# The w_down load behind the first gated turn, in two tiles of seven and three row tiles; one store of the last slab whole

## The chip, the cores and the metric

The kernel runs on one core of a Trainium2 chip. The metric is the device time of one execution in microseconds (us). A profile is one execution recorded by the hardware profiler; its span runs from the first to the last instruction.

## What is computed

The input x has 2048 tokens of 512 numbers. It is normalised, and the normalised tokens go two ways: through a diagonal complex linear recurrence over the tokens (an S5 layer with 512 states), and through a gated feed-forward network with 1376 hidden columns. The two results are multiplied and added to x.

```python
xn = layernorm(x)
# S5: h_t = Lam_bar * h_(t-1) + B_bar @ xn_t ;  y = 2 Re(C h) + xn * Dskip
s = A(xn, Lambda, B, C, log_dt, Dskip)
# feed-forward: (gelu(xn @ w_gate) * (xn @ w_up)) @ w_down
g = silu(B(xn, w_gate, w_up, w_down))
out = x + s * g
```

## The kernel before

The tokens are worked on in four slabs of 512 (`NS`), each with four row tiles of 128 tokens (`M`). All weights stay in SBUF: `wg`, `wu` (4 x 128 input rows by 1376 columns), `wd` (11 row tiles of 128 hidden rows, the last with 96, by 512 columns), `BT` and `C2` for the recurrence.

For a row tile, TensorE multiplies by `w_up` and `w_gate` in three column chunks of 512, 512 and 352 (`first_w` in the first slab, `gate_tile`, line 450, in the others); ScalarE takes the results out of PSUM (gelu for the gate), and VectorE multiplies the two into `at` (128 tokens x 1408 columns, `first_at`, lines 445 and 447, in the first slab). A DMA transpose, here called a turn (`at_t`, line 479), writes `at` to `atT` with the hidden index on the partitions. `down_pair` (line 485) then runs eleven matmuls for a row tile over the eleven row tiles of `wd` (line 495), and ScalarE applies silu into `g2` (line 498).

For the recurrence, `half` (line 551) does half of the states of a slab: TensorE multiplies `BT` with the turned normalised tokens `xnT` (line 561), ScalarE copies the results into `U` (line 563), and VectorE rotates, scans (line 592) and rotates back into `hst`. `y_tile` (lines 511 to 527) multiplies `hst` with `C2`, then VectorE multiplies by `g2`, adds x into `ot`, and SP stores the tile. The stores of the last slab's first two row tiles are cut into two halves of 256 columns (line 525).

`norm` (line 759) loads slab s (for s of 2 and 3 through `load_slab`, line 217) and normalises it: ScalarE forms sums (line 774) and writes the normalised tile `xna` (line 779), and one turn for the slab writes `xnT` (line 378).

PSUM has six ring banks, which `bank()` hands out in turn as the steps are built, and two `ybank`s. A matmul group that gets a bank waits until the engine that reads the bank's earlier content is done.

Every piece of work is a numbered step of a `Plan`. A step says what it reads and writes, from which its predecessors follow; its number is its place in the order of building. The list `ORDER` at the head of the file is the order in which steps are issued, written out by hand, and so fixes the order on each engine. All DMAs are issued by SP, in the order of the list, into one hardware queue. In the stretch that matters SP's steps are: turn of `xna` for the first slab, the two turns of `B` into `BT` (steps 15 and 16), `w_down`'s main load of 10 row tiles (step 121, line 695), the turns of the gated row tiles 0, 2 and 1 (steps 160, 162, 161), the turn of the second slab's `xna` (232), the load of the third slab of x (279), the turn of row tile 3 (163), and the two turns of `C` (204, 205). `w_down`'s eleventh row tile (96 rows, step 122, line 696) is loaded early, between weights and the second slab of x.

Of the kernel before, what the change touches and what calls it, by code (L numbers as in the profile page):

```python
# [17 lines left out]
PE, ACT, DVE, POOL, SP = "PE", "ACT", "DVE", "POOL", "SP"  # L18
# [1 line left out]

ORDER = (
# [23 lines left out]
)  # L45


# [33 lines left out]
def kernel(  # L81
# [17 lines left out]
    nc = tc.nc  # L99
    P = 128  # L100
    S = 2048
    D = 512
    F = 1376
# [5 lines left out]
    NS = S // TS  # L109
    M = TS // P  # L110
    NFT = (F + P - 1) // P
    FP = NFT * P
    FL = F - (NFT - 1) * P
    CH = [(0, 512), (512, 1024), (1024, F)]
    HD = D // 2
# [12 lines left out]
    def sb(name, shape, dt=BF16):  # L128
        return consts.tile(shape, dt, name=name)
# [2 lines left out]
    xnT = sb("xnT", [P, 2, M, KT, P])  # L132
    wg = sb("wg", [P, KT, F])
    wu = sb("wu", [P, KT, F])
    wd = sb("wd", [P, NFT, D])
    BT = sb("BT", [P, 2, KT, D])
    C2 = sb("C2", [P, 2, NPT, D])
    pv = sb("pv", [P, P])
# [3 lines left out]
    atT = sb("atT", [P, NFT, TS])  # L142
# [42 lines left out]
    def pe(n, cols, emit, reads=(), writes=(), **kw):  # L185
        return pl.add(PE, n * (cols + 6) / 2400.0, emit, reads, writes, lag=0.22, **kw)
# [4 lines left out]
    def dma(eng, issue, land, emit, reads=(), writes=(), **kw):  # L191
        return pl.add(eng, issue, emit, reads, writes, lag=land, **kw)
# [292 lines left out]
    def down_pair(s, h):  # L485
        gi = g2_n[0] % NG2
        g2_n[0] += 1
        for b in range(2):
            m = 2 * h + b
            r, ps = bank()  # L490

            def f(m=m, ps=ps):
                for k in range(NFT):
                    fs = min(P, F - k * P)
                    T.matmul(ps[:], lhsT=atT[:fs, k, m * P : (m + 1) * P], rhs=wd[:fs, k, :], start=(k == 0), stop=(k == NFT - 1))  # L495
            pe(NFT, 512, f, [("atT", m), "wd0", "wd"], [("bank", r)])
            g2s[s, m] = (gi, b)
            acts(512, lambda b=b, ps=ps: act(out=g2[gi][:, b, :], in_=ps[:], func=AF.Silu), [("bank", r)], [("g2", gi, b)], table="silu", rank=3.0)  # L498

# [2 lines left out]
    def y_part(s, m, c0, c1, bank, key, seed, e):  # L502

        w = c1 - c0
        ps = bank[:, 0:w]
        if seed:
            acts(w, lambda: act(out=ps, in_=sk[s % 2][:, m, c0:c1], func=AF.Copy), [("sk", s % 2, m)], [key])  # L507

        def f():
            for j in range(2 * NPT):  # L510
                T.matmul(ps, lhsT=hst[s % 2][:, j // NPT, j % NPT, m * P : (m + 1) * P], rhs=C2[:, j // NPT, j % NPT, c0:c1],  # L511
                         start=(j == 0 and not seed), stop=(j == 2 * NPT - 1), skip_group_check=True)
        pe(2 * NPT, w, f, [("hst", s % 2, 0), ("hst", s % 2, 1)] + C2S + ([key] if seed else []), [key])
        gi, b = g2s[s, m]
        if seed:
            dve(w, lambda: V.tensor_tensor(out=yg[e][:, c0:c1], in0=ps, in1=g2[gi][:, b, c0:c1], op=ALU.mult), [key, ("g2", gi, b)], [("yg", e, c0)])  # L516
        else:
            ys = tF[:, 0, c0:c1]
            dve(w, lambda: V.tensor_tensor(out=ys, in0=ps, in1=sk[s % 2][:, m, c0:c1], op=ALU.add), [key, ("sk", s % 2, m)], [("tF",)])
            dve(w, lambda: V.tensor_tensor(out=yg[e][:, c0:c1], in0=ys, in1=g2[gi][:, b, c0:c1], op=ALU.mult), [("tF",), ("g2", gi, b)], [("yg", e, c0)])  # L520
        o = 2 + m % 2 if s == NS - 1 and m >= M - 2 else m % 2
        dve(w, lambda: V.tensor_tensor(out=ot[o][:, c0:c1], in0=yg[e][:, c0:c1], in1=x_tok[:, s * M + m, c0:c1], op=ALU.add),  # L522
            [("yg", e, c0), ("x", s, m)], [("ot", o, c0)], rate=2.0)
        mg = s * TS + m * P
        cuts = (0, HD) if (NS - 1, 0) <= (s, m) < (NS - 1, M - 2) else (c0,)
        for lo, hi in zip(cuts, (*cuts[1:], c1)):
            dma(SP, 0.35, 1.5, lambda lo=lo, hi=hi: nc.sync.dma_start(out=out_td[mg : mg + P, lo:hi], in_=ot[o][:, lo:hi]), [("ot", o, c0)], [("out", s, m, lo)], svc=(2, 0.4, 0.9))

# [163 lines left out]
            first_at(m)  # L692
    load_slab(1, after=sp_last)
    wd_r = B_w_down[0 : (NFT - 1) * P, :].rearrange("(k p) d -> p k d", p=P)
    dma(SP, 0.6, 6.7, lambda: nc.sync.dma_start(out=wd[:, 0 : NFT - 1, :], in_=wd_r), writes=["wd0"], after=sp_last, svc=(2, 3.7, 1.0))
    dma(SP, 0.5, 4.0, lambda: nc.sync.dma_start(out=wd[:FL, NFT - 1, :], in_=B_w_down[(NFT - 1) * P : F, :]), writes=["wd"], after=sp_last, svc=(2, 0.3, 1.0))
    dma(SP, 0.7, 3.0, lambda: nc.sync.dma_start(out=Drow[:], in_=A_Dskip.partition_broadcast(P)), writes=["Drow"], after=sp_last, svc=(2, 0.5, 1.0))
    tables()
    for m in range(M):
# [156 lines left out]
```

## Time and profile before

| | us |
|---|---|
| median of three runs (lowest, highest) | 179.38 (179.35, 179.89) |
| the profiled execution | 179.31 |
| its span | 177.5 |
| VectorE busy in the span | 157.5 |
| ScalarE busy in the span | 123.9 |

The profiled execution's own time is 1.8 us more than its span. In the rows of the profile, PE is TensorE's matmuls, PEld its weight loads, DVE is VectorE, ACT ScalarE, POOL GpSimd, and SPq the issue of DMAs by SP. A row of the timeline has the start, the duration, the engine, the line and the operation, the tiles (out<-in), the count of instructions merged into it, and in brackets the idle time of the engine before it with what ended that. A DMA's row there is its issue; the transfer goes on after it. "us to landing" is from the start of the issue to the last byte's signal.

Up to 44 us the queue of DMAs is busy without a long break: weights, turns and three slabs of x go through it. Behind that there are stretches with no transfer at all.

### The profile page before, as it was taken

The page shows a single profiled execution, that of the slowest core. Times are in us where ns is not written, and L with a number is a line of the kernel's source. Part 1 is how long each engine was busy: PE and PEld are TensorE (multiplying, and loading weights), DVE is VectorE, ACT ScalarE, POOL GpSimd, SP SyncE. Part 2 cuts the span into 40 slices and gives each one's busy share as a digit, 9 for nine tenths or more (in the row PEclk, how much of TensorE's full clock was granted, in tenths as well). Part 3 has the DMA queues.
Part 4 walks back from the last instruction along what each step waited for, and adds up shares of the span by engine and source line. Part 5 has one row for each costly group of instructions (what it writes and reads, how often), then busy time and mean ns, then how long its engine had stood idle before and what let it go on. Part 6 is the DMA issues. An engine that isn't in the chain of part 4 may idle for free.

```text
span 177.5 us, 2427 instructions
## 1 busy us (share of the span) xinstructions
PE 172.5 (97%) x846; PEld 82.3 (46%) x846; DVE 157.5 (89%) x256; ACT 123.9 (70%) x238; POOL 11.3 (6%) x26
## 2 busy tenths in 40 slices
PE   8999999899999999999999999999999999999992
PEld 3455453344455544444445454444444455444451
DVE  3678999999699994999979999899999999999754
ACT  6689989839999999899578855373148618572240
POOL 2472030000200000000040000000000000000000
PEclk9999999999999999999999999999999999999999
DMA  5999999999000709414000064094000006626122
GB/s 164 286 344 229 177 264 227 214 265 212 0 0 0 197 3 185 99 61 80 0 0 6 24 135 101 30 192 85 0 0 0 0 30 144 83 52 140 37 62 77
DMA packets 48355, 18.66 MB, mean 105 GB/s; under 512 B 40312, under 2 KB 47832, under 8 KB 48344
## 3 DMA queue, kind: packets, MB, share of 16 engines
q1 hardware_dynamic: 48344, 18.52, 47.7%
q8 instruction: 6, 0.10, 0.2%
q14 instruction: 5, 0.04, 0.1%
HBM read 6.46 MB, written 2.10 MB: 48 GB/s over the span
## 4 chain that ended last, share of the span: by engine, by line
PE 84%; DVE 7%; DMA 5%; POOL 2%; issue 0%; DVEq 0%
PE ring L463 31%; PE ring L495 22%; PE ybank L511 15%; PE ring L561 12%; DMA atT<-at 5%; PE ring L402 2%; DVE st L281 2%; DVE Q L650 1%; PE ring L300 1%; DVE yg L516 1%; DVE tab L650 1%; POOL dt__137 L618 1%; PE ybank L300 1%; DVE junk L522 1%; POOL rho L622 1%; POOL rs L293 0%
## 5 line engine op out<-in xcount | busy, mean ns | idle before, releaser
L463 PEld LDWEIGHTS <-xnT 128*128 128x128 bf16 x288 | 28.2, 98 | 28.4
L495 PE MATMUL ring<-wd,atT 128*128 128x512 bf16 (+1 forms) x176 | 39.4, 379 | 1.1 <-DMA atT<-at 1.1
L463 PE MATMUL ring<-wg,xnT 128*128 128x512 bf16 (+1 forms) x144 | 31.6, 357 | 0.0
L463 PE MATMUL ring<-wu,xnT 128*128 128x512 bf16 (+1 forms) x144 | 31.3, 357 | 0.0
L561 PE MATMUL ring<-xnT,BT 128*128 128x512 bf16 x128 | 30.1, 379 | 0.0
L592 DVE TENSOR_TENSOR_SCAN Fs<-rho,ini,W 128x512 bf16<-128x512 f32 x24 | 29.7, 1272 | 0.1
L466 ACT ACTIVATE ub<-ring 128x512 bf16<-128x512 f32 (+1 forms) x36 | 19.2, 555 | 13.7 <-PE ring L463 13.5
L511 PE MATMUL ybank<-C,hst 128*128 128x512 bf16 x120 | 27.7, 379 | 0.0
L495 PEld LDWEIGHTS <-atT 128*128 128x128 bf16 (+1 forms) x176 | 17.1, 98 | 22.1 <-DMA atT<-at 1.5
L563 ACT ACTIVATE U<-ring 128x512 bf16<-128x512 f32 x32 | 18.1, 599 | 7.3 <-PE ring L561 7.3
L466 ACT ACTIVATE gt<-ring 128x512 bf16<-128x512 f32 (+1 forms) x36 | 19.5, 556 | 3.7 <-PE ring L463 3.5
L498 ACT ACTIVATE g<-ring 128x512 f32<-128x512 f32 x16 | 9.4, 594 | 15.5 <-PE ring L495 15.3
L511 PEld LDWEIGHTS <-hst 128*128 128x128 bf16 x136 | 13.3, 98 | 14.0
L561 PEld LDWEIGHTS <-BT 128*128 128x128 bf16 x128 | 12.5, 98 | 14.8
L573 DVE TENSOR_TENSOR Q<-U,tab 128x4096 bf16<-128x4096 bf16 x8 | 18.3, 2289 | 0.9 <-ACT tab L657 0.7
L573 DVE TENSOR_TENSOR Q<-Fs,tab 128x4096 bf16<-128x4096 bf16 x8 | 18.3, 2288 | 0.1
L516 DVE TENSOR_TENSOR yg<-ybank,g 128x512 bf16<-128x512 f32 x15 | 10.2, 685 | 5.8 <-PE ybank L511 5.7
L774 ACT ACTIVATE junk<-x_tok 128x512 bf16<-128x512 bf16 x16 | 10.0, 632 | 1.3 <-DMA x_tok<-in_A_x_dram 1.3
L507 ACT ACTIVATE ybank<-sk 128x512 f32<-128x512 bf16 x15 | 9.1, 604 | 1.7 <-DVE yg L516 1.6
L779 ACT ACTIVATE xna<-x_tok,nb,rs 128x512 bf16<-128x512 bf16 x12 | 9.5, 812 | 0.0
L592 DVE TENSOR_TENSOR_SCAN Fs<-rho,W 128x512 bf16<-128x512 f32 x8 | 9.3, 1211 | 0.1
L472 DVE TENSOR_TENSOR at<-gt,ub 128x1024 bf16<-128x1024 bf16 x12 | 8.2, 684 | 0.0
(149 smaller groups left out, 172.0 us busy)
## 6 DMA issues: line engine op xcount, KB each, us to landing
x_tok<-in_A_x_dram SPq DMA_DIRECT2D x3, 512.0 KB, 4.2
out_dram<-ot SPq DMA_DIRECT2D x12, 128.0 KB, 2.1
wd<-in_B_w_down_dram SPq DMA_DIRECT2D x1, 1280.0 KB, 7.9
wu<-in_B_w_up_dram SPq DMA_DIRECT2D x4, 256.0 KB, 3.5
wg<-in_B_w_gate_dram SPq DMA_DIRECT2D x1, 864.0 KB, 8.0
x_tok<-in_A_x_dram SPq DMA_DIRECT2D x4, 128.0 KB, 4.2
wg<-in_B_w_gate_dram SPq DMA_DIRECT2D x1, 512.0 KB, 5.9
wu<-in_B_w_up_dram SPq DMA_DIRECT2D x1, 352.0 KB, 5.0
```

What stands on the lines that cost most here:

```text
L463: T.matmul(ps[:, 0 : b - a], lhsT=xnT[:, s % 2, m, k, :], rhs=wt[:, k, a:b], start=(k == 0), stop=(k == KT - 1))
L466: acts(b - a, lambda: act(out=dst[:, a:b], in_=ps[:, 0 : b - a], func=AF.Copy if up else AF.Gelu_apprx_tanh), [("bank", r)], [key], table= ...
L495: T.matmul(ps[:], lhsT=atT[:fs, k, m * P : (m + 1) * P], rhs=wd[:fs, k, :], start=(k == 0), stop=(k == NFT - 1))
L498: acts(512, lambda b=b, ps=ps: act(out=g2[gi][:, b, :], in_=ps[:], func=AF.Silu), [("bank", r)], [("g2", gi, b)], table="silu", rank=3.0)
L511: T.matmul(ps, lhsT=hst[s % 2][:, j // NPT, j % NPT, m * P : (m + 1) * P], rhs=C2[:, j // NPT, j % NPT, c0:c1], start=(j == 0 and not seed ...
L516: dve(w, lambda: V.tensor_tensor(out=yg[e][:, c0:c1], in0=ps, in1=g2[gi][:, b, c0:c1], op=ALU.mult), [key, ("g2", gi, b)], [("yg", e, c0)])
L561: T.matmul(ps[:], lhsT=BT[:, ri, k, pt * P : (pt + 1) * P], rhs=xnT[:, s % 2, :, k, :], start=(k == 0), stop=(k == KT - 1))
L563: acts(512, lambda q=q, ri=ri, ps=ps: act(out=U[ui][:, ri, q, :], in_=ps[:], func=AF.Copy), [("bank", r)], [("U", ui, q, ri)])
L573: dve(4096, lambda: V.tensor_tensor(out=Qf, in0=src.unsqueeze(1).to_broadcast(WQ), in1=table, op=ALU.mult), reads, ["Q"], rate=2.0)
L592: pl.add(DVE, 1.12 if s == 0 else 1.185, lambda ri=ri, q=q, pt=pt, first=first: V.tensor_tensor_scan(out=Fs[:, ri, q, :], data0=rho[:, pt ...
L774: acts(512, lambda i=i, fn=fn, sc=sc, m=m: act(out=junk()[:], in_=x_tok[:, s * M + m, :], func=fn, scale=sc, accum_out=sx[:, s, i, m : m + ...
L779: acts(512, lambda m=m: act(out=xn[m], in_=x_tok[:, s * M + m, :], func=AF.Identity, scale=rs[:, s, m : m + 1], bias=nb[:, s, m : m + 1]), ...
```

## The change

Three things are edited.

- `wd` becomes two SBUF tiles: `wd0` with the row tiles 0 to 6, `wd1` with 7 to 10. The matmul of a down projection takes row tile k from the one or the other.
- The main load of `w_down` (row tiles 0 to 9, 1280 KB) becomes two DMAs, of seven row tiles (896 KB) into `wd0` and of three (384 KB) into `wd1`. In `ORDER` they stand directly behind the turn of the first gated row tile, where the old load stood directly before it. The load of the eleventh row tile goes into `wd1` and stays where it was.
- The store of the last slab's first row tile is one DMA of 512 columns in place of two of 256.

One step is added and one taken away, so all numbers from 122 to 655 move up by one in `ORDER`. Apart from that the order differs only in the places of the load and of the store that is gone. The two lines of the list around the load, before and after, and the other hunks:

```diff
-    15, 164, 168, 183, 165, 169, 228, 233, 16, 121, 166, 170, 185, 187, 167, 189, 231, 171, 230, 229, 184, 186, 362, 190, 188, 172, 173, 174, 176,
-    175, 177, 178, 179, 180, 181, 182, 191, 160, 237, 238, 162, 241, 242, 161, 239, 232, 245, 247, 262, 279, 287, 284, 283, 280, 286, 248, 263, 240,
+    15, 165, 169, 184, 166, 170, 229, 234, 16, 167, 171, 186, 188, 168, 190, 232, 172, 231, 230, 185, 187, 363, 191, 189, 173, 174, 175, 177, 176,
+    178, 179, 180, 181, 182, 183, 192, 161, 121, 122, 238, 239, 163, 242, 243, 162, 240, 233, 246, 248, 263, 280, 288, 285, 284, 281, 287, 249, 264,
...
-    wd = sb("wd", [P, NFT, D])
+    KW = 7
+    wds = sb("wd0", [P, KW, D]), sb("wd1", [P, NFT - KW, D])
...
-                    T.matmul(ps[:], lhsT=atT[:fs, k, m * P : (m + 1) * P], rhs=wd[:fs, k, :], start=(k == 0), stop=(k == NFT - 1))
-            pe(NFT, 512, f, [("atT", m), "wd0", "wd"], [("bank", r)])
+                    T.matmul(ps[:], lhsT=atT[:fs, k, m * P : (m + 1) * P], rhs=(wds[0][:fs, k, :] if k < KW else wds[1][:fs, k - KW, :]), start=(k == 0), stop=(k == NFT - 1))
+            pe(NFT, 512, f, [("atT", m), "wd0", "wd1", "wd"], [("bank", r)])
...
-        cuts = (0, HD) if (NS - 1, 0) <= (s, m) < (NS - 1, M - 2) else (c0,)
+        cuts = (0, HD) if (NS - 1, 1) <= (s, m) < (NS - 1, M - 2) else (c0,)
...
-    dma(SP, 0.6, 6.7, lambda: nc.sync.dma_start(out=wd[:, 0 : NFT - 1, :], in_=wd_r), writes=["wd0"], after=sp_last, svc=(2, 3.7, 1.0))
-    dma(SP, 0.5, 4.0, lambda: nc.sync.dma_start(out=wd[:FL, NFT - 1, :], in_=B_w_down[(NFT - 1) * P : F, :]), writes=["wd"], after=sp_last, svc=(2, 0.3, 1.0))
+    for i, (k0, k1) in enumerate(((0, KW), (KW, NFT - 1))):
+        dma(SP, 0.6, 6.7, lambda i=i, k0=k0, k1=k1: nc.sync.dma_start(out=wds[i][:, 0 : k1 - k0, :], in_=wd_r[:, k0:k1, :]), writes=[f"wd{i}"], after=sp_last, svc=(2, 1.9, 1.0))
+    dma(SP, 0.5, 4.0, lambda: nc.sync.dma_start(out=wds[1][:FL, NFT - 1 - KW, :], in_=B_w_down[(NFT - 1) * P : F, :]), writes=["wd"], after=sp_last, svc=(2, 0.3, 1.0))
```

40 rows, old and new, of the table ORDER are left out of this document.

## The prediction, made before the result was known

> **What bounds the kernel now.** I read the page first, then the chain of waits, then the stages around the place that is edited, then the queues of the engines there.
>
> ```profile
> span 177.5 us, 2427 instructions
> PE 172.5 (97%) x846; PEld 82.3 (46%) x846; DVE 157.5 (89%) x256; ACT 123.9 (70%) x238; POOL 11.3 (6%) x26
> DMA  5999999999000709414000064094000006626122
> ```
>
> TensorE (PE) is busy for 172.5 of 177.5 us, so a gain has to come from the few places where it stands still, and what is gained there has to survive to the end. The 16 DMA engines are full in the first ten slices (to 44 us), and the edited load lies in that stretch. The chain shows one transfer on the path:
>
> ```profile
> 22.66 9.24 DMA atT<-at
> 31.91 0.05 issue
> 31.95 7.31 PE ring L495 x33
> ...
> 41.85 2.38 PE ring L495 x11
> ```
>
> The first turn of a gated row tile (`at` to `atT`) is issued at 22.66 and lands at 31.91; then the first down projections start. The stages give the size of the hole:
>
> ```profile
> 24.50:30.90 6.40, 6.40 (x30) 2.72 (x28) 6.29 (x12) 5.45 (x10) 0.13 (x1) 1.00 1.08 256
> 30.90:31.95 1.05, 0.00 (x0) 0.00 (x0) 1.05 (x2) 1.05 (x3) 0.00 (x0) 1.00 1.22 126
> 31.95:38.85 6.90, 6.90 (x32) 3.15 (x33) 6.76 (x7) 3.66 (x6) 0.00 (x0) 1.00 1.09 249
> 38.85:48.28 9.43, 9.43 (x45) 4.28 (x44) 7.54 (x13) 9.43 (x24) 1.01 (x1) 1.00 0.61 132
> 48.28:54.10 5.82, 5.82 (x32) 2.89 (x30) 5.79 (x9) 5.71 (x11) 0.00 (x0) 1.00 0.00 0
> 54.10:65.50 11.40, 11.40 (x60) 5.73 (x59) 11.32 (x18) 11.30 (x20) 0.00 (x0) 1.00 0.31 78
> ```
>
> Columns: stretch, its length, busy time of PE, weight loads, VectorE, ScalarE and GpSimd with their counts, clock, DMA share, GB/s. PE does nothing for 1.05 us, and is full before and after. ScalarE (fourth busy column) is the other thing to see: 3.66 of 6.90 us up to 38.85, then 9.43 of 9.43, 5.71 of 5.82 and 11.30 of 11.40.
>
> **Why the turn is late.** SP's queue and the landing times:
>
> ```profile
> 21.98 0.58 SPq L695 DMA_DIRECT2D wd<-in_B_w_down_dram  x1
> 22.66 9.59 SPq L479 DMA_TRANSPOSE atT<-at  x3
> 32.34 2.23 SPq L378 DMA_TRANSPOSE xnT<-xna  x1
> 34.63 0.94 SPq L217 DMA_DIRECT2D x_tok<-in_A_x_dram  x1
> ```
>
> ```profile
> 22.66 5.57 SPq L479 DMA_TRANSPOSE atT<-at  x1
> ```
>
> ```profile
> 28.33 2.40 SPq L479 DMA_TRANSPOSE atT<-at  x1
> ```
>
> ```profile
> L479 SPq DMA_TRANSPOSE atT<-at x16: 1262/1396/5568, 22.7 to 159.8; - x16
> ```
>
> ```profile
> x_tok<-in_A_x_dram SPq DMA_DIRECT2D x3, 512.0 KB, 4.2
> out_dram<-ot SPq DMA_DIRECT2D x12, 128.0 KB, 2.1
> wd<-in_B_w_down_dram SPq DMA_DIRECT2D x1, 1280.0 KB, 7.9
> ...
> atT<-at SPq DMA_TRANSPOSE x16, 3.7
> out_dram<-ot SPq DMA_DIRECT2D x4, 64.0 KB, 1.6
> ```
>
> The `w_down` load is issued at 21.98 and lands 7.9 us later, at 29.9. The turn behind it holds SP for 5.57 us against a median of 1.40, and lands 9.2 us after issue against 3.7. So it stood behind 1280 KB in the same queue. The second turn, behind it, still holds SP for 2.40.
>
> **The change, part by part.** *The load goes behind the first turn.* The turn's row tile is ready in time:
>
> ```profile
> 21.13 0.34 DVE L447 TENSOR_TENSOR at<-gt,at 128x352 bf16<-128x352 bf16 x1
> ...
> 25.68 0.33 DVE L447 TENSOR_TENSOR at<-ub,at 128x352 bf16<-128x352 bf16 x1
> ```
>
> The first tile's last product ends at 21.47, so SP issues the turn at 21.98, in the place of the load. With 3.7 us from issue to landing it lands at 25.7. The two loads are issued at about 23.4 and 24.0 (1.40 for the turn, then 0.58 each). They replace one issue by two; the extra 0.6 us lies where SP has to wait anyway, since the second turn needs the tile that is ready at 26.01 and is then held by the full queue as the first one was. Without that cover it would cost 0.6 us of SP.
>
> The queue's work is only reordered. What is moved ahead of `w_down` is one turn; I take its 1.40 us of issue as its share of the queue (bounds: 1.26, the shortest issue, and 2.0, the time from the load's landing at 29.9 to the turn's at 31.9). The load's 7.9 us from 21.98 then end at 29.9 + 1.4 = 31.3. The last three row tiles are 384 KB; at the 249 GB/s of the stretch from 31.95 they take 1.6 us (an estimate; 2.4 at the most, three tenths of 7.9), so the first seven land at about 29.7.
>
> *The split into seven and three.* A down projection's eleven matmuls take 2.38 us (chain, 0.216 each), so seven take 1.51. PE is free at 30.90, needs the first seven row tiles then and has them since 29.7; it needs the other three at 32.4 and has them since 31.3. The 1.05 us of waiting go. The second turn becomes the one that stands behind the load, landing 2.0 us after it, at 33.3, where PE wants it at 30.9 + 2.38 = 33.3; bounds 0 and 0.6 (with 2.0 in place of 1.4 above). No matmul is added, and the two tiles are read at the same cost.
>
> *What is late next.* ScalarE has its own start time:
>
> ```profile
> 38.85 0.63 ACT L774 ACTIVATE junk<-x_tok 128x512 bf16<-128x512 bf16 x1 [1.34 <-DMA x_tok<-in_A_x_dram]
> ...
> 52.90 0.63 ACT L563 ACTIVATE U<-ring 128x512 bf16<-128x512 f32 x1
> ```
>
> ```profile
> 53.90 0.55 PEld L463 LDWEIGHTS <-xnT 128*128 128x128 bf16 x4
> ```
>
> It idles 1.34 us for the slab of x whose load was issued at 34.63, starts at 38.85, and has 15.14 us of work in the 15.25 us to 54.10. That work is in a fixed order and does not begin earlier because PE is earlier. It empties the six ring banks: the `U` copy at 52.90 ends at 53.53 and frees the bank into which PE's 352-wide up group writes from 53.90. So PE had 0.37 us of slack there; with the 0.05 us that a release takes in the chain, 0.32. Of the 1.05 us PE can keep about 0.3 at 54 us, unless the slab lands earlier too. VectorE's scan output, the next meeting point, leaves more:
>
> ```profile
> 64.23 0.69 DVE L581 TENSOR_TENSOR hst<-Q 128x1024 bf16<-128x1024 bf16 x1
> ```
>
> ```profile
> 65.36 1.11 PEld L511 LDWEIGHTS <-hst 128*128 128x128 bf16 x6
> ```
>
> It ends at 64.92 and PE reads it from 65.36: 0.44. Behind 66 us ScalarE's long waits are for PE, so that it moves along:
>
> ```profile
> ACT ub L466 <- PE ring L463: 13.5, 9, 2.9
> ```
>
> *The slab's landing.* Behind `w_down` stood three turns, then the turn of `xna`, then the slab; now two turns stand there. The load ends 1.4 later, and one turn's issue (1.52 with its gap: from 28.33 + 2.40 to 22.66 + 9.59 in SP's rows) is gone from behind it. So the slab moves by 1.4 - 1.5 = -0.1 us; with the bounds 1.26 and 2.0, by -0.25 to +0.5. ScalarE's stretch moves with it, one to one.
>
> *The store.* Before:
>
> ```profile
> 170.39 2.48 SPq L527 DMA_DIRECT2D out_dram<-ot  x4
> 173.85 1.66 SPq L527 DMA_DIRECT2D out_dram<-junk  x3
> ```
>
> The first of four issues disappears into its twin. A whole store lands at 170.39 + 2.1 = 172.5, two halves at about 172.4; the last store is issued at 175.18, when its VectorE add is done. Cover gone, it would be worth 0.4 us of SP at most; I take 0, bounds -0.1 and +0.1.
>
> **The sum.** Gain = 0.3 (the slack) + 0.1 (the slab) = 0.4 us, from 0.32 - 0.5 = -0.2 to 0.37 + 0.25 = 0.6. Against the profiled execution, 179.31 us (a span of 177.5 and 1.8 around it): 178.9. The median, 179.38, lies 0.07 higher; I say 179.0 us, own range 178.7 to 179.6.
>
> **The rivals.** *The whole wait is gained.* In the queue there is a hole that the stages show:
>
> ```profile
> 30.80:31.60 0.80, 0.10 (x1) 0.00 (x0) 0.80 (x2) 0.80 (x3) 0.00 (x0) 1.00 1.22 78
> ```
>
> 78 GB/s against 249 in the neighbouring stretch, 0.55 us lost among the turns. If it is swallowed while plain loads are in flight, the slab lands 0.1 + 0.55 = 0.65 us earlier, and PE keeps 0.3 + 0.65 or nearly the full 1.05: 178.4. For it: the hole falls into the load's time now. Against it: SP's issue, not the packets, seems to pace the turn of `xna` and the slab behind it.
>
> *A dearer second load (slower).* If each load is followed by a pause that the queue pays serially, all behind the second one is late. The nearest row for such a price is a 64 KB store, 1.6 us from issue to landing, mostly not its bytes. Then the slab lands at 38.83 + 1.6 - 0.1 and ScalarE's stretch is 1.5 late; the 0.3 of slack takes its part: 179.4 + 1.2 = 180.6. It decides as soon as the pause is over 0.4 us. Against it: the DMA share stays over 1 in every stretch from 24.5 to 38.85, across loads and turns. The Trainium skill, "DMA: Bandwidth & Descriptors", section "Rules for kernel authors", speaks against the split: at least 1 MiB per DMA for full bandwidth, and 1280 KB becomes 896 and 384. Its "Specifications" give about 0.6 us to the first byte on SP's path; paid serially that would make 179.6, an estimate from that page.
>
> *The wait only changes its name.* If the engines take the two loads unevenly and the seven tiles land with the three, or the load moves later by more than the turn's 1.4 us, PE waits for `w_down` at 30.9 to 31.9 instead of for the turn: the gain is 0 and with the slab's upper bound the loss 0.5, 179.4 to 179.9. Against it: 1.2 us of margin for the seven tiles.
>
> **How the numbers follow.** ScalarE-bound gain 0.45, whole wait 0.33, dearer load 0.11, renamed wait 0.11. The 0.3% that a measurement of this kernel can tell from no change is 0.54 us. Faster by more: nine tenths of the second case and a fifth of the first, 0.38; slower by more: the third, a third of the last and the edge of the first, 0.16; within: 0.46. The range 178.3 to 180.0 leaves out the dearer load and the outer edge of the whole wait.
>
> **What would show it.** Right: the first turn is issued near 22.0 and lands near 26; PE runs through 30.9; ScalarE still starts its statistics near 38.8 and is full to 54; PE shows a short wait for ScalarE between 50 and 54. The second case would show the slab landing before 38.3. Wrong: a PE wait for `wd`, SP held much longer than to 29.7 by the second turn, or the slab landing after 39.2.

## The result, and the profile after

| | us |
|---|---|
| before, median of 20 executions (lowest, highest) | 179.64 (178.91, 180.44) |
| after, median of 20 executions (lowest, highest) | 178.67 (178.11, 179.57) |
| ratio after / before, 95% interval | 0.9951 [0.9935, 0.9967] |
| the profiled execution after, and its span | 179.25, 177.5 |

The change makes the kernel faster by 0.49%, that is by 0.88 us (0.59 to 1.17: the interval times 179.64). The forecast was 179.0 us, a gain of 0.4. The time is inside the range, the sign is right, the gain is twice what was forecast. The forecast was reckoned from a median of 179.38; from the 179.64 measured beside the change it would read 179.24. That 178.67 lies in the range says little, since the range of 178.3 to 180.0 holds both medians of the kernel before as well; the gain of 0.88 is beyond the 0.6 that the bounds of the sum allowed. A gain over 0.3% (0.54 us), which is what came, had a chance of 0.38 in the forecast; a change within 0.3% had 0.46.

The page of the changed kernel, first its span, its busy times and the DMA row:

```profile
span 177.5 us, 2426 instructions
PE 173.5 (98%) x846; PEld 82.9 (47%) x846; DVE 157.4 (89%) x256; ACT 123.8 (70%) x238; POOL 11.2 (6%) x26
DMA  5997999999000709514000064094000006626112
```

The span is that of before to a tenth, though the medians differ by almost a microsecond. PE is busy for 1.0 us more and idle for 1.0 us less. Of the added busy time 0.91 us lies within the first 10 us, with no matmul more: the first gate pieces of the chain, 14 matmuls, end at 8.02 us before and at 8.93 after. The chain of waits, in pieces of start, duration, engine and line, shows where:

```profile
24.90 6.91 PE ring L562 x32
31.81 7.13 PE ring L496 x33
38.94 2.59 PE ring L562 x12
...
50.55 15.07 PE ring L464 x76
65.62 1.73 PE ybank L512 x8
```

The transfer `atT<-at` is gone from the chain: the down projections (L496) follow the 32 recurrence matmuls (L562) without a gap. But these 32 end at 31.81, where before they ended at 30.90. Everything up to there came 0.91 us later in this execution, before any part of the change could act on PE. The same pieces of the kernel before, behind its wait:

```profile
50.87 14.80 PE ring L463 x76
65.68 1.73 PE ybank L511 x8
```

From the end of those 32 matmuls, which I call F from here on, to the first `y` product there are 65.68 - 30.90 = 34.78 us before and 65.62 - 31.81 = 33.81 after. Counted from F the change gains 0.97 us, and the late head of this one execution hides 0.91 of it. The L464 piece is 0.27 us longer than before, which is taken up below.

The stages, cut at the same events as before (stretch, its length, busy time of PE, weight loads, VectorE, ScalarE, GpSimd, then clock, DMA share and GB/s):

```profile
24.90:31.81 6.91, 6.91 (x34) 3.14 (x32) 6.80 (x13) 5.98 (x11) 0.64 (x1) 1.00 1.00 263
31.81:39.12 7.31, 7.31 (x36) 3.32 (x34) 7.17 (x8) 4.72 (x9) 0.00 (x0) 1.00 1.09 243
39.12:48.55 9.43, 9.43 (x46) 4.26 (x44) 8.19 (x13) 9.43 (x24) 1.01 (x1) 1.00 0.63 131
48.55:54.12 5.57, 5.57 (x29) 2.67 (x28) 5.54 (x8) 5.54 (x9) 0.00 (x0) 1.00 0.00 0
54.12:65.50 11.38, 11.38 (x61) 5.71 (x59) 11.35 (x18) 11.38 (x21) 0.00 (x0) 1.00 0.32 78
30.80:31.60 0.80, 0.80 (x5) 0.38 (x4) 0.80 (x3) 0.80 (x3) 0.00 (x0) 1.00 1.25 203
```

PE stands still in none of them. The stretch 30.80 to 31.60, where the queue moved 78 GB/s before, moves 203 now; `w_down` is in flight there. That is so in this execution: the section on the forecast comes back to it. ScalarE is again full from its first sum on (39.12) to the end of the table: 9.43 of 9.43, 5.54 of 5.57, 11.38 of 11.38.

SP's queue:

```profile
23.40 1.41 SPq L480 DMA_TRANSPOSE atT<-at  x1
24.85 1.46 SPq L697 DMA_DIRECT2D wd<-in_B_w_down_dram  x2
26.96 5.67 SPq L480 DMA_TRANSPOSE atT<-at  x2
32.72 1.87 SPq L379 DMA_TRANSPOSE xnT<-xna  x1
34.63 1.09 SPq L218 DMA_DIRECT2D x_tok<-in_A_x_dram  x1
```

The first turn now takes 1.41 us of SP and lands 3.6 us after its issue (9.2 before). The two turns behind the loads hold SP for 5.67 us together; three held it for 9.59 before. ScalarE's start, and three copies that free banks for PE:

```profile
39.12 0.63 ACT L776 ACTIVATE junk<-x_tok 128x512 bf16<-128x512 bf16 x1 [1.92 <-DMA x_tok<-in_A_x_dram]
...
49.86 0.60 ACT L467 ACTIVATE gt<-ring 128x512 bf16<-128x512 f32 x1
...
50.83 1.09 ACT L564 ACTIVATE U<-ring 128x512 bf16<-128x512 f32 x2
...
53.17 0.62 ACT L564 ACTIVATE U<-ring 128x512 bf16<-128x512 f32 x1
```

```profile
53.85 1.12 PEld L464 LDWEIGHTS <-xnT 128*128 128x128 bf16 x7 [0.16 <-issue]
```

This is the short wait for ScalarE that the forecast named: the copy ends at 53.17 + 0.62 = 53.79, and the next weights of the up group are loaded at 53.85, after a pause. The profile puts the pause down to "issue", not to ScalarE; only the times side by side show it. It is the last and smallest of three such places. PE's weight loads of the gate group start at 50.51 and 51.49, where the gate copy ended at 50.46 and the first of the two `U` copies at 51.43: each time 0.05 or 0.06 us behind ScalarE. Counted from F, the loads at 50.51, 51.49 and 53.85 come 0.11, 0.23 and 0.27 us later than in the third profile of this kernel below, in which PE does not wait. So 0.23 of the 0.27 us is lost in the gate group, and 0.04 at the place that the forecast named.

The stores at the end:

```profile
167.14 5.67 SPq L528 DMA_DIRECT2D out_dram<-ot  x5
173.80 1.65 SPq L528 DMA_DIRECT2D out_dram<-junk  x3
```

The last three stores take 1.65 us of SP, against 1.66 before.

### The profile page after: what moved, and what is told of

It is laid out like the page before. It is cut to its first block, busy times and chain, and to the rows that moved or that the text cites. A ratio compares the mean times of both kernels' runs of the same rounds, so it can differ in the third digit from the quotient of the medians.

```text
span 177.5 us, 2426 instructions
## 1 busy us (share of the span) xinstructions
PE 173.5 (98%) x846; PEld 82.9 (47%) x846; DVE 157.4 (89%) x256; ACT 123.8 (70%) x238; POOL 11.2 (6%) x26
## 4 chain that ended last, share of the span: by engine, by line
PE 97%; DVE 1%; issue 0%; DVEq 0%
PE ring L464 32%; PE ring L496 21%; PE ring L562 16%; PE ybank L512 15%; PE ring L433 5%; PE ring L403 3%; PE ybank L433 2%; PE ring L301 1%; DVE yg L517 1%; DVE junk L523 1%; PE ybank L301 1%; PE ybank L330 0%; PE ring L315 0%; PE ring L305 0%; PE ring L330 0%
## 5 line engine op out<-in xcount | busy, mean ns | idle before, releaser
L464 PEld LDWEIGHTS <-xnT 128*128 128x128 bf16 x288 | 28.1, 98 | 28.7 <-issue 0.6
L496 PE MATMUL ring<-wd,atT 128*128 128x512 bf16 (+1 forms) x176 | 39.3, 379 | 0.0
L464 PE MATMUL ring<-wg,xnT 128*128 128x512 bf16 (+1 forms) x144 | 31.7, 357 | 0.0
L464 PE MATMUL ring<-wu,xnT 128*128 128x512 bf16 (+1 forms) x144 | 31.3, 357 | 0.0
L562 PE MATMUL ring<-xnT,BT 128*128 128x512 bf16 x128 | 30.1, 379 | 0.0
L496 PEld LDWEIGHTS <-atT 128*128 128x128 bf16 (+1 forms) x176 | 17.2, 98 | 20.8
L562 PEld LDWEIGHTS <-BT 128*128 128x128 bf16 x128 | 12.5, 98 | 14.7
```

The source lines that it names most:

```text
L464: T.matmul(ps[:, 0 : b - a], lhsT=xnT[:, s % 2, m, k, :], rhs=wt[:, k, a:b], start=(k == 0), stop=(k == KT - 1))
L496: T.matmul(ps[:], lhsT=atT[:fs, k, m * P : (m + 1) * P], rhs=(wds[0][:fs, k, :] if k < KW else wds[1][:fs, k - KW, :]), start=(k == 0), st ...
L562: T.matmul(ps[:], lhsT=BT[:, ri, k, pt * P : (pt + 1) * P], rhs=xnT[:, s % 2, :, k, :], start=(k == 0), stop=(k == KT - 1))
```

## The experiments

Every kernel was timed against the kernel before on the same chip. The ratios are to that kernel, with 95% intervals. Where a profile is read, it is read from F, since the head alone moves by about 1 us from one execution to the next. A profile is one execution, and not always a usual one of its kernel.

**The changed kernel again, and its parts.** The first four kernels shared their runs of the kernel before (median 179.84 us).

The changed kernel, unaltered:

> The changed kernel once more, for a second profile of it. Theory 1 (the forecast's: the turn no longer stands behind w_down, and ScalarE, which starts its sums when the third slab of x lands, takes part of the gain back between 50 and 55 us): TensorE runs through the first down projections without a wait; the slab lands 13.7 to 14.4 us after the second BT turn; TensorE loses up to 0.3 us for ScalarE between 50 and 55 us where the slab is late, and nothing where it is early. Time 0.994 to 0.997 of before. Rival (the whole wait carries, ScalarE plays no part): no stall at all between 50 and 55 us, 0.994.

Measured: 178.79 us, ratio 0.9953 [0.9927, 0.9979], span 176.6. F is 31.25, ScalarE's first sum starts at 37.93, the first `y` product at 64.79: 33.54 us from F.

```profile
24.34 6.91 PE ring L562 x32
31.25 1.94 PE ring L496 x9
...
64.79 0.43 PE ybank L512 x2
```

So the gain repeats, and in this execution the loss of 0.27 us is gone as well.

One load of 1280 KB in one tile, moved behind the first turn; the stores as before:

```diff
-    ... 228, 233, 16, 121, 166, 170, ... 182, 191, 160, 237, 238, ...
+    ... 228, 233, 16, 166, 170, ... 182, 191, 160, 121, 237, 238, ...
```

> w_down's main load stays one DMA into one tile but stands behind the first gated turn; the stores as before. If the place in the queue is what counts (theory 1): all or nearly all of the gain, 0.994 to 0.997 of before, since in the changed kernel's profile the last part of w_down (31.75 us) landed just as TensorE came to it (31.81). If the split into seven and three row tiles is needed as the forecast held: TensorE waits for wd by up to 0.5 us, 0.996 to 0.999.

Measured: 179.08 us, ratio 0.9976 [0.9947, 1.0005], span 177.0. PE's timeline, with the idle time before a row and what ended it in brackets:

```profile
23.95 7.07 PE L561 MATMUL ring<-xnT,BT 128*128 128x512 bf16 x32
31.40 4.92 PE L495 MATMUL ring<-wd,atT 128*128 128x512 bf16 x21 [0.38 <-DMA wd<-in_B_w_down_dram]
```

PE has its turned row tile and waits for `wd`: the whole load ends after F. Here the rival "the wait only changes its name" is seen, at a third of the old wait. The first `y` product starts 65.11 - 31.02 = 34.09 us after F, 0.55 later than at best. In these two profiles the move gives about 0.7 us of the 1.24 that the kernel before loses there. The time alone would not show it: its interval reaches no change. That the split is worth the rest rests on this wait, not on the two times, whose intervals overlap.

Two loads into two tiles, still ahead of the first turn; the stores as before (the order is shown against the changed kernel):

```diff
-    ... 16, 167, 171, ... 182, 183, 192, 161, 121, 122, 238, 239, ...
+    ... 16, 121, 122, 167, 171, ... 182, 183, 192, 161, 238, 239, ...
```

> w_down's load as seven and three row tiles into two tiles, still ahead of the first gated turn; the stores as before. Theory 1: the turn lands as late as before, TensorE waits about 1 us for it, 0.999 to 1.001. If a second load costs the queue a serial pause (the forecast's slower rival), the turn lands 0.5 to 1.6 us later: 1.003 to 1.009. If the split itself brings the gain: 0.995.

Measured: 179.94 us, ratio 1.0013 [0.998, 1.0047], span 178.5. SP's queue and PE's wait:

```profile
22.57 1.19 SPq L697 DMA_DIRECT2D wd<-in_B_w_down_dram  x2
23.86 9.09 SPq L480 DMA_TRANSPOSE atT<-at  x3
```

```profile
32.70 3.63 PE L496 MATMUL ring<-wd,atT 128*128 128x512 bf16 x15 [1.18 <-DMA atT<-at]
```

The three turns again hold SP for 9 us and PE waits for the first: 1.18 where it was 1.06 in the same view of before. By the trace's DMA records the slab lands 9.06 us after the end of the loads (8.93 before). A second load has no price that a run of this size can tell, and the rival that gave it 1.6 us falls. The Trainium skill, "DMA: Bandwidth & Descriptors", section "Rules for kernel authors", asks for at least 1 MiB per DMA where full bandwidth is the goal; with 896 and 384 KB in a queue that is full anyway no loss is seen here.

Only the store of the last slab's first row tile whole:

```diff
-        cuts = (0, HD) if (NS - 1, 0) <= (s, m) < (NS - 1, M - 2) else (c0,)
+        cuts = (0, HD) if (NS - 1, 1) <= (s, m) < (NS - 1, M - 2) else (c0,)
```

> Only the store of the last slab's first row tile is one DMA in place of two. Theory 1: 0.999 to 1.001, SP has free time there and the last store waits for VectorE. If the store has a part in the gain: 0.998 or below.

Measured: 179.79 us, ratio 0.9998 [0.9968, 1.0029]. The store is worth nothing, as forecast. In its profile F is 31.69, 0.8 us later than in the profile of the kernel before, while the turn lands only 0.07 later (31.98); so PE waits less, and 0.52 us are lost from F instead of 1.24. A late head hides part of the old wait. A late head alone can thus make single executions of the two kernels come out alike.

**Is ScalarE's start the limit?** The forecast held that PE can keep only what the slab's landing allows. The slab can be made late alone, with nothing else changed: the turn of row tile 3, which SP issues directly behind the slab's load, is put directly ahead of it. Once in the changed kernel:

```diff
-    ... 246, 248, 263, 280, 288, ... 289, 290, 164, 244, ...
+    ... 246, 248, 263, 164, 280, 288, ... 289, 290, 244, ...
```

> The changed kernel with the turn of row tile 3 ahead of the load of the third slab of x, so that the slab lands some 1.4 us later; nothing that TensorE waits for itself comes later. Theory 1 (ScalarE's stretch starts with the slab, and TensorE follows it through the ring banks): the slab lands about 15.4 us after TensorE's first matmul on BT in place of 13.7 to 14.4, ScalarE's sums start with it, TensorE stalls 1.0 to 1.5 us in the stretch of the second slab's gate and up products (between 45 and 60 us), and the gain is lost: 1.000 to 1.004 of before. Rival (ScalarE plays no part): 0.995, no stall.

and once in the kernel before:

```diff
-    ... 245, 247, 262, 279, 287, ... 288, 289, 163, 243, ...
+    ... 245, 247, 262, 163, 279, 287, ... 288, 289, 243, ...
```

> The same swap in the kernel before. Theory 1: TensorE's wait for the first turn stays at about 1.1 us, the slab lands about 16.5 us after the first BT matmul, less that wait 15.4, and TensorE stalls a further 1.0 to 1.4 us behind: 1.005 to 1.008. Rival: 1.000.

Measured (kernel before on this chip 179.7 us): the changed kernel with a late slab 180.22 us, ratio 1.0047 [1.0022, 1.0072]; the kernel before with a late slab 181.32 us, ratio 1.0103 [1.0073, 1.0132]. ScalarE's start and two of PE's rows in the changed kernel with a late slab:

```profile
39.77 0.63 ACT L776 ACTIVATE junk<-x_tok 128x512 bf16<-128x512 bf16 x1 [3.44 <-DMA x_tok<-in_A_x_dram]
```

```profile
47.23 1.02 PE L464 MATMUL ring<-wu,xnT 128*128 128x512 bf16 x4 [0.53 <-ACT U L564]
...
51.15 2.60 PE L464 MATMUL ring<-wg,xnT 128*128 128x512 bf16 x12 [0.29 <-ACT gt L467]
```

and the same in the kernel before with a late slab:

```profile
42.05 0.63 ACT L774 ACTIVATE junk<-x_tok 128x512 bf16<-128x512 bf16 x1 [3.66 <-DMA x_tok<-in_A_x_dram]
```

```profile
49.52 1.02 PE L463 MATMUL ring<-wu,xnT 128*128 128x512 bf16 x4 [0.53 <-ACT U L563]
53.43 2.60 PE L463 MATMUL ring<-wg,xnT 128*128 128x512 bf16 x12 [0.29 <-ACT gt L466]
```

PE now waits for ScalarE by name, at the same steps in both. Moving one turn ahead of the slab takes the whole gain and more, so the limit is real. Both kernels came out slower than expected, since the slab moved by more than the 1.4 us that were put down for the turn: against F by 1.94 us from the mean of the three profiles of after, and by 2.67 from the profile of before. The limit can be written as one rule. Let S be the start of ScalarE's first sum, W the wait at the first down projection, and 33.54 us the shortest time from F to the first `y` product. Then the loss against 33.54 is W plus what S - F - W has over a fixed number of about 7.04 us. In the changed kernel with a late slab S - F is 39.77 - 30.94 = 8.83, so 1.79 is forecast by the rule; the first `y` product at 66.26 gives 66.26 - 30.94 - 33.54 = 1.78. In the other S - F is 42.05 - 31.43 = 10.62 and W is 1.56, so 1.56 + 2.02 = 3.58; measured 68.54 - 31.43 - 33.54 = 3.57. A ScalarE that plays no part would have given 0 and 1.56.

| profile | F | W | S - F | lost by the rule | lost (first `y` - F - 33.54) |
|---|---|---|---|---|---|
| before | 30.90 | 1.21 | 7.95 | 1.21 | 1.24 |
| the split alone | 31.53 | 1.33 | 8.15 | 1.33 | 1.35 |
| the store alone | 31.69 | 0.50 | 7.17 | 0.50 | 0.52 |
| the move alone | 31.02 | 0.54 | 7.59 | 0.55 | 0.55 |
| after, first profile | 31.81 | 0 | 7.31 | 0.27 | 0.27 |
| after, second | 31.25 | 0 | 6.68 | 0 | 0 |
| after, third (last run below) | 30.99 | 0 | 6.69 | 0 | 0.01 |

W is counted from F to the start of the down projections as they lie in the pipeline, 0.16 us more than PE's idle row; 7.04 is fitted to the first profile of after, and the two kernels with a late slab were not used for it. Each row is one execution; the first profile of after is among the slower of its twenty (179.25 us, median 178.67), the third is the fastest of its ten. The span adds nothing new: from the first `y` product to its end there are 111.8 to 112.1 us in all of these.

**Can the slab come still earlier?** If 0.27 us are lost in some executions, an earlier slab should give them back. Three kernels tried it. In the first the slab's load is issued ahead of the turn of `xna`:

```diff
-    ... 162, 240, 233, 246, 248, 263, 280, 288, ...
+    ... 162, 240, 280, 233, 246, 248, 263, 288, ...
```

> The changed kernel with the load of the third slab of x ahead of the turn of the second slab's xna. Theory 1: ScalarE's sums start 1.8 us earlier and no stall is left between 45 and 60 us (worth 0 to 0.3 us); the turn of xna lands that much later, 13.8 to 14.3 us after the first BT matmul where TensorE wants it at 14.0, which costs 0 to 0.3 us. 0.993 to 0.997. Rival: 0.995 plus the wait for xnT alone.

Measured: 178.59 us, ratio 0.9947 [0.9928, 0.9967]. ScalarE starts at 37.77, 5.88 us after F, but the waits list names a new one:

```profile
PEld L562 <- DMA xnT<-xna: 1.2, 1, 1.2
```

The turn of `xna` stood behind the slab's 512 KB and is late for the next recurrence matmuls; 0.88 us are lost from F. In this execution the wait has moved from ScalarE to PE itself. This execution took 179.97 us, the longest of the twelve, against a median of 178.59, so that a usual one can hardly lose as much.

In the second the slab is loaded as two DMAs, of the row tiles 2 and 3 and then 0 and 1, in the order in which ScalarE reads them:

```diff
-        dma(SP, 0.8, 4.0, lambda: nc.sync.dma_start(out=x_tok[:, s * M : (s + 1) * M, :], in_=x_r[:, s * M : (s + 1) * M, :]),
-            writes=[("x", s, m) for m in range(M)], svc=SLAB, **kw)
+        for a, b in ((2, 4), (0, 2)) if s == 2 else ((0, M),):
+            dma(SP, 0.8, 4.0, lambda a=s * M + a, b=s * M + b: nc.sync.dma_start(out=x_tok[:, a:b, :], in_=x_r[:, a:b, :]),
+                writes=[("x", s, m) for m in range(a, b)], svc=SLAB, **kw)
```

> The changed kernel with the third slab of x loaded as two DMAs, its row tiles 2 and 3 first, since ScalarE's first sums are of these. Theory 1: ScalarE's sums start 0.6 to 1.0 us earlier against the first BT matmul (13.0 to 13.6), nothing else comes later, and no stall is left: 0.9935 to 0.996, at or a little under the changed kernel. If a further DMA costs the queue a serial pause, what stands behind it lands 0.5 us or more later, without an effect on TensorE.

Measured: 178.95 us, ratio 0.9969 [0.9948, 0.9989]. In the third, of these two halves the first goes ahead of the turn of `xna` and the second stays behind it, and one of ScalarE's sums of the early half moves up (the diff is against the second):

```diff
-    ... 240, 233, 246, 248, 263, 280, 281, 289, 286, 285, 282, 288, ...
+    ... 240, 280, 233, 246, 248, 263, 281, 289, 286, 288, 285, 282, ...
```

> The changed kernel with the third slab of x as two DMAs: row tiles 2 and 3 ahead of the turn of the second slab's xna, row tiles 0 and 1 behind it; ScalarE's three sums of row tiles 2 and 3 that came first or fifth now stand first. Theory 1: ScalarE's sums start about 12 us after the first BT matmul, the turn of xna lands 0.9 us later than in the changed kernel (12.8 to 13.4, wanted at 14.0), TensorE has no wait and no stall between the first down projection and 65 us: from the first BT matmul to the first y product 40.45 us, as in the best profile so far. 0.993 to 0.996 of before. If a further DMA or the moved half makes another transfer late (the second C turn, as with the slab in halves behind the turn): a stall of up to 0.5 us, 0.996 to 0.998.

Measured: 178.91 us, ratio 0.9935 [0.9906, 0.9965], the kernel before 180.26 on this chip. ScalarE in the two kernels, first with both halves behind the turn:

```profile
46.88 1.15 ACT L748 ACTIVATE tF<-hst,cim 128x1024 f32<-128x1024 bf16 x1 [0.84 <-DMA hst<-in_A_C_im_dram]
```

and with one half ahead of it:

```profile
36.08 0.62 ACT L777 ACTIVATE junk<-x_tok 128x512 bf16<-128x512 bf16 x1
...
46.33 1.15 ACT L748 ACTIVATE tF<-hst,cim 128x1024 f32<-128x1024 bf16 x1 [1.40 <-DMA hst<-in_A_C_im_dram]
```

ScalarE starts its sums 5.28 us after F in the last (36.08 - 30.80), over 2 us sooner than in the first profile of after, and then waits 1.40 us for the second turn of `C`, which SP issues behind the slab (the last section takes this wait apart). Lost from F: 0.46 and 0.69 us. None of the three is told apart from the changed kernel. That had to be so where it has nothing left to lose, as the last run shows, the changed kernel a third time, on the chip of the one before:

> The changed kernel again, on the same chip as the run beside it, for a third profile. Theory 1: no wait for the first turn or for wd; a stall of 0 to 0.3 us between 45 and 60 us, as large as ScalarE's start after the first BT matmul exceeds 14.1 us. 0.994 to 0.997.

Measured: 178.75 us, ratio 0.9919 [0.9892, 0.9946], span 176.4. Its chain and ScalarE's start:

```profile
24.09 6.91 PE ring L562 x32
30.99 7.13 PE ring L496 x33
...
49.74 14.80 PE ring L464 x76
64.54 1.73 PE ybank L512 x8
```

```profile
37.68 0.63 ACT L776 ACTIVATE junk<-x_tok 128x512 bf16<-128x512 bf16 x1 [1.30 <-DMA x_tok<-in_A_x_dram]
```

The L464 piece is back at 14.80 us, and from F to the first `y` product there are 33.55. In two of three profiles the changed kernel keeps the whole wait that it removed.

## Why the forecast was half of the gain

**The wait and the first turn: right.** In the third profile of after the turn is issued at 22.16 and lands at 26.14 (forecast 22.0 and 25.7), in the first, with its late head, at 23.40 and 27.0. PE runs through F in all three.

**The two loads: right, with more room for the second than forecast.** Counted from F, the forecast had the seven row tiles 1.2 us ahead and the three 0.4 behind. By the trace's DMA records they land at 30.70 and 31.75 in the first profile of after (F 31.81) and at 29.67 and 30.71 in the third (F 30.99): 1.1 and 1.3 us ahead for the seven, 0.1 and 0.3 ahead for the three. The second turn was put at 2.4 us after F, just when it is needed; it lands at 33.09 and 32.04, 1.3 and 1.05 after F.

**ScalarE as the next limit, with 0.3 us of slack: right.** By the rule above the kernel before has 7.04 - (7.95 - 1.21) = 0.30 us of slack; 0.32 was read from the `U` copy and the weight load behind it, and of the three places where PE follows ScalarE in the first profile of after this one has the least slack in the kernel before (the other two have 0.47 and 0.35, with the 0.05 for the release taken off). The two kernels with a late slab show the one-to-one dependence that the forecast used, and the first profile of after the wait itself.

**The failing step: "the slab moves by 1.4 - 1.5 = -0.1 us", with bounds of -0.25 and +0.5.** Against F it moved by 7.31 - 7.95 = -0.64 us in the first profile and by 6.68 - 7.95 = -1.27 in the two others, beyond the bound. F carries the scatter of the head (with the old order S - F is 7.95, 8.15 and 7.17 in the three profiles of the table), so the terms are better read within the queue. There both were mis-sized, in the same direction:

| us | before, split alone, store alone | after (three profiles), move alone |
|---|---|---|
| second turn of `B` landed to end of the `w_down` load | 5.46, 5.73, 4.98 | 6.40, 6.30, 6.16, 6.51 |
| end of that load to the slab's landing | 8.93, 9.06, 8.85 | 7.35, 6.92, 6.95, 7.23 |

The load ends 0.95 us later for the turn ahead of it (the means, 6.34 - 5.39), where 1.40 was taken; the queue behind the load is 1.84 us shorter for one turn less (8.95 - 7.11), where 1.52 was taken. A turn's issue time on SP was used as its share of the queue in both places. It is dearer behind the load than ahead of it. The landings one by one show where: with the old order the three turns behind the load land 4.65, 4.81 and 4.54 us after it, the first of them alone 2.0; with the new order the two turns take 2.5 to 2.8 us and the first 1.2 to 1.3. The turn of `xna` and the slab together take about the same in both (4.3 and 4.4). Together the two terms are 0.89 us earlier; against F the mean of the three profiles of after, 6.89, is 0.87 below the mean of the three with the old order, 7.76. The move alone has the same two numbers as the full change, so it is the order, not the split, that shortens the queue. The two kernels with a late slab agree: one turn more ahead of the slab made the stretch from the load's end to the slab 1.9 us longer in the changed kernel (8.93) and 2.2 in the kernel before (11.15). What in the queue makes the first turn behind the load so dear with the old order stays open; that the difference of some 0.9 us is there, in four profiles against three, is shown.

With 0.3 of slack and the slab 0.64 to 1.27 us earlier in place of 0.1, PE keeps 0.94 us or the full wait. From F the lost time is 1.24, 1.35 and 0.52 us in three profiles with the old order, mean 1.04, and 0.27, 0 and 0.01 in the three of after, mean 0.09: a gain of 0.95, beside the 0.88 [0.59, 1.17] of the times.

**The rivals.** "The whole wait is gained" was nearest: it named a slab 0.65 us earlier, and its sign, a landing before 38.3, is there in two of the three profiles of after (37.91 and 37.66; 39.10 in the first, with its late head). Its mechanism, that the hole in the queue is filled by plain loads, is not borne out as the common cause: the first profile of after has no such hole, but the third moves 126 GB/s from 29.90 to 30.70, and the move alone 29 GB/s from 30.40 to 31.20, while `w_down` has still to land. The reason against it, that SP's issue paces the turn of `xna` and the slab, did not keep the slab late: SP's issue moves up itself (the slab's load is issued at 33.39 in the third profile of after, 2.4 us after F, and at 34.63 before, 3.7 after). That a full queue holds SP there is a reading of its issue times (2.23 and 1.91 us for this turn of `xna`, 1.48 for an earlier one), not shown apart. "A dearer second load" falls with the split alone, "the wait only changes its name" holds for one undivided load and not for two.

**The store: right,** 0.9998 [0.9968, 1.0029].

## What to carry to other kernels

A small transfer on which an engine waits should not stand behind a big load in the same queue when the load is needed later; and a transfer's issue time is a poor measure of its share of the queue: here the landing behind the big load moved by 0.9 us where issue times gave 0.1. After removing a wait, look for the engine that starts by a transfer of its own, and find out by delaying that transfer alone whether it is the limit. Compare two profiles from an event that the change cannot touch, not from zero: here two spans of 177.5 us hid a gain of 0.97 us behind a head that came 0.91 us later.

## What was not expected

**The head moves by a microsecond.** F lies between 30.80 and 31.89 in twelve profiles with nearly the same code up to there, and both orders of the loads have early and late ones. In the chains of the first and third profile of after the difference arises within the first 10 us: the first gate pieces are `5.18 3.74 PE ring L403 x14` in the one and `4.87 3.24 PE ring L403 x14` in the other. What makes the early loads differ was not tried.

**A turn's signal can come well after its bytes.** In the kernels with a divided slab ScalarE went on at 46.88 and 46.33, though the second turn of `C` had moved its data by 44.78 and 44.25. A turn signals sixteen times here, and the wait needs them all. Fifteen signals came by 45.23 and 44.70, before ScalarE was free (46.04 and 44.93), the sixteenth at 46.80 and 46.24: both waits are for this one alone. In the DMA records the turn's last two packets, of 4 bytes, start only at 45.70 and 45.05, just as a 16 KB packet of another queue, called "instruction", ends (44.78 to 45.72 and 43.95 to 45.07). The kernel with the slab ahead of the turn of `xna` shows the same (46.42 beside 45.35 to 46.43, and a wait of 0.64 us). In the nine other profiles no packet of the turn comes late, though in one of them, the store alone, the two overlap by 0.27 us as well. That the 16 KB packet held the two small ones back on one DMA engine is thus read from the times of three executions: the records do not name the engine, and no run takes it apart. It would mean that the losses of 0.46 and 0.69 us are not the divided slab's own.
